# Two state-space convolutions mixed by a gate: the kernels' transform split 64 by 32, doubled rows for one product operation, the gate applied to the inverse's output, the input's spectrum stored once

## The chip, the core and the metric

The kernel runs on one core of a Trainium2 chip. The metric is device time in microseconds (us). Five engines work from queues of their own, each in program order: PE multiplies matrices (the trace shows its weight loads apart, as PEld), DVE and ACT work on vectors and read PE's results in PSUM, POOL works on vectors in SBUF alone, and SP issues every DMA. An engine waits on semaphores for the others, and whatever stands behind a waiting instruction in its queue waits too.

## The reference, cut

Both branches convolve the same input, 2048 positions of 512 channels, with a kernel of 2048 taps that is built from 128 states per channel. A sigmoid of one sum over the channels mixes them.

```python
x = A_u
g = _sigmoid((x * gate_w).sum(-1, keepdims=True))
# branch A (B is alike, with 2 C dt in place of C dt B)
logdA = dt * (A_re + 1j * A_im)
P = jnp.exp(logdA[:, :, None] * l[None, None, :])
K = jnp.einsum("dn,dnl,dn->dl", Cc, P, dB).real
y = irfft(rfft(u, 2 * L) * rfft(K, 2 * L), 2 * L)[:, :, :L] + u * Dskip
...
return g * a + (1 - g) * b
```

## The kernel before

The 512 channels are worked on as eight groups `v` of 64, each with both branches (`k` is 0 or 1); two groups make a quarter `q`. A group takes these steps.

- **Tables** (`chunk`, eight times a group, 16 channels of one branch each). POOL makes the angles `x` (L561, L552) and the magnitudes `E` (L572, L580). ACT takes the sine and the cosine into the PSUM tiles `sd` (L592, L593, L594). DVE multiplies them into `QD` and `E` (L600, L605, L615, L610). PE sums over the 128 states (`products`, L631): per channel 32 by 64 values, four channels side by side in one bank of `ps`. ACT copies two chunks' sums into `K` (L653).
- **The kernel's transform.** `put` is the first stage, a sum over 32 rows per channel (L674), copied into `F` by ACT or DVE (L686). `forward` is the second, over 64 values, with the constant `c_g` (L697).
- **The product** with the input's spectrum `U`: two DVE operations on 128x512, L769 and L772, of which the second takes real and imaginary parts swapped and a sign.
- **The inverse's first stage**: for each frequency column two matmuls that add up, L781 and L782; ACT copies the sum to `st` (L785), and SP stores it to DRAM as `wt` (L788).
- **The inverse's second stage** (`final`, once a quarter): SP loads `wt` back (L803), PE multiplies by `wb` and `wg` (L814), the result is copied (L823 or L825) and stored (L826).

The input's own transform runs once, near the start (`stage1_u`, `stage2_u`): `put` and `forward` for four quarters, then two stores of 128 and 64 rows to `ud` in DRAM (L739), so that a load of `U` (L760) can fetch both row orders. `gate` sums the input over the channels (L843, 512 columns at a time, the same sum in all 128 rows), applies the sigmoid (L854), and POOL multiplies the inverse's constant weights by it (`wg`, L861) and by one minus it (`wb`, L873).

The order on each engine is made before the launch by a planner (`Plan.run`): every operation has an assumed cost and a due time, and whenever an engine is free in the plan, the ready operation with the earliest due time is put next, if the buffers it needs are free in the plan. Due times come from tables (`TO`, `LAG`, `FSP` and others), buffers from `SLOTS`: in PSUM two tiles `sd` of two banks each, for sine and cosine alone, and four banks `ps` for all else.

## Time and profile before

| What | Value |
|---|---|
| Three runs | 503.86 us median, 503.26 to 507.71 |
| The profiled execution | 506.61 us, its span 504.8 us |
| PE, DVE, ACT, POOL busy in the span | 422.9, 398.2, 388.8, 393.8 us |
| DMA, mean | 169 GB/s, 85.45 MB |

An engine's busy time counts a moment once, however many of its instructions overlap. On PE they overlap heavily, so a group's mean duration times its count exceeds its busy time; what a burst costs is read from the starts in the timeline. The trace shows each f32 matmul of the program as two records, each with a weight load of its own: L781 has 256 matmuls in the program and 512 records. The chain of waits goes back from the last instruction, at each step to what released it.

### The profile page before, as it was taken

Reading aid. Unit: us, or ns where it says so; the run is one execution under the profiler, and the core shown is the slowest. Engines: PE = TensorE matmul, PEld = TensorE weight load, DVE = VectorE, ACT = ScalarE, POOL = GpSimd, SP = SyncE. Lnnn points to the kernel's source line nnn. Section 1 sums busy time; section 2 is a strip of 40 time slices with the busy share of each in tenths; the row PEclk is TensorE's granted clock in tenths of the full one; section 3 lists DMA queues with packets and bytes.
Section 4 is the critical chain, followed back from the end, with each engine's and each line's share of the span. In section 5 each row is a group of like instructions: output and inputs, shape, how many; then the busy total and the mean of one; then the engine's idle time right before and its main releaser. Section 6 shows DMA issues by size and latency. Waiting matters only on the chain.

```text
span 504.8 us, 21830 instructions
## 1 busy us (share of the span) xinstructions
PE 422.9 (84%) x9584; PEld 383.2 (76%) x9584; DVE 398.2 (79%) x564; ACT 388.8 (77%) x598; POOL 393.8 (78%) x365
## 2 busy tenths in 40 slices
PE   3497996788989999998289986598999899799946
PEld 3397895777767898888279875488989799789936
DVE  5748998989939889999859988978979999863420
ACT  4659989789999887799998778857999878562111
POOL 4674997979969999989898999768979999920000
PEclk9999997699999999999669999789999999989988
DMA  8958773254654455444208676347336157753954
GB/s 284 382 159 270 225 222 122 86 181 117 153 171 130 138 185 149 127 128 128 62 7 248 197 236 214 107 139 219 106 114 195 34 157 229 218 156 115 307 164 189
DMA packets 69438, 85.45 MB, mean 169 GB/s; under 512 B 4704, under 2 KB 50144, under 8 KB 69088
## 3 DMA queue, kind: packets, MB, share of 16 engines
q1 hardware_dynamic: 69344, 84.06, 53.5%
q8 instruction: 75, 1.23, 1.0%
q14 instruction: 19, 0.16, 0.1%
HBM read 50.49 MB, written 33.59 MB: 167 GB/s over the span
## 4 chain that ended last, share of the span: by engine, by line
PE 45%; ACT 20%; DMA 15%; DVE 8%; issue 7%; POOL 3%; SPq 1%; DVEq 0%; ACTq 0%; POOLq 0%
PE ps L697 10%; PE ps L631 8%; PE ps L781 7%; PE ps L782 7%; PE ps L674 6%; PE ps L814 5%; DMA wt<-st 4%; DMA c_g<-in_c_g 3%; DMA X<-wt 3%; ACT sd L592 3%; ACT sd L594 2%; ACT x L593 2%; DMA AB<-in_prm 2%; ACT st L785 2%; DVE z L772 2%
## 5 line engine op out<-in xcount | busy, mean ns | idle before, releaser
L580 POOL TENSOR_TENSOR E<-AB 128x1024 f32<-128x1024 f32 x64 | 125.4, 1960 | 0.1
L781 PE MATMUL ps<-z,c_t 128*128 128x128 f32 x512 | 102.6, 282 | 3.7 <-DVE z L772 1.6
L782 PE MATMUL ps<-z,c_t 128*128 128x128 f32 x512 | 99.9, 277 | 1.2 <-DVE z L772 0.8
L600 DVE TENSOR_TENSOR QD<-sd,E 128x1024 f32<-128x1024 f32 x64 | 77.8, 1216 | 20.3 <-ACT sd L592 9.4
L631 PE MATMUL ps<-E 128*32 128x64 f32 x2048 | 68.1, 230 | 24.5 <-DVE E L610 17.5
L697 PE MATMUL ps<-F,c_g 128*128 128x128 f32 x640 | 85.7, 281 | 3.5 <-ACT F L686 1.3
L781 PEld LDWEIGHTS ps<-z,c_t 128*128 128x128 f32 x512 | 77.6, 191 | 9.0 <-DVE z L772 3.3
L697 PEld LDWEIGHTS ps<-F,c_g 128*128 128x128 f32 x640 | 77.4, 191 | 8.0 <-ACT F L686 1.6
L782 PEld LDWEIGHTS ps<-z,c_t 128*128 128x128 f32 x512 | 77.7, 192 | 2.8 <-DVE z L772 2.7
L631 PEld LDWEIGHTS ps<-E 128*32 128x32 f32 x2048 | 50.9, 115 | 36.5 <-issue 18.9
L561 POOL TENSOR_TENSOR x<-pi,c_tm 128x512 int32<-128x512 int32 x64 | 68.0, 1064 | 13.1 <-ACT sd L594 12.0
L610 DVE TENSOR_TENSOR E<-sd,E 128x1024 f32<-128x1024 f32 x64 | 77.6, 1213 | 0.8 <-ACT sd L594 0.8
L572 POOL TENSOR_TENSOR E<-AB 128x512 f32<-128x512 f32 x64 | 68.5, 1072 | 8.7 <-issue 2.8
L592 ACT ACTIVATE sd<-x 128x1024 f32<-128x1024 int32 x64 | 65.9, 1030 | 9.0 <-DVE QD L605 7.6
L785 ACT COPY st<-ps 128x512 f32<-128x512 f32 x64 | 37.5, 586 | 44.3 <-PE ps L782 25.1
L552 POOL TENSOR_TENSOR x<-gh 128x512 int32<-128x512 int32 x64 | 68.7, 1074 | 0.2
L593 ACT ACTIVATE x<-x 128x1024 f32<-128x1024 int32 x64 | 67.8, 1060 | 1.3
L594 ACT ACTIVATE sd<-x 128x1024 f32<-128x1024 f32 x64 | 66.0, 1032 | 2.6 <-DVE E L615 0.9
L631 PE MATMUL ps<-QD 128*32 128x64 f32 x2048 | 67.1, 228 | 0.1
L769 DVE TENSOR_TENSOR z<-ps,U 128x512 f32<-128x512 f32 x64 | 43.8, 684 | 27.1 <-PE ps L697 23.7
L631 PEld LDWEIGHTS ps<-QD 128*32 128x32 f32 x2048 | 53.0, 116 | 0.0
L674 PE MATMUL ps<-w,K 64*64 64x64 f32 x2048 | 41.0, 230 | 9.0 <-DVE fi L454 3.4
(118 smaller groups left out, 748.9 us busy)
## 6 DMA issues: line engine op xcount, KB each, us to landing
U<-ud SPq DMA_DIRECT2D x32, 512.0 KB, 4.1
wt<-st SPq DMA_DIRECT2D x64, 256.0 KB, 2.7
X<-wt SPq DMA_DIRECT2D x26, 512.0 KB, 5.6
ud<-z SPq DMA_DIRECT2D x32, 256.0 KB, 3.4
U<-in_u SPq DMA_DIRECT2D x16, 256.0 KB, 4.2
ud<-z SPq DMA_DIRECT2D x32, 128.0 KB, 3.4
U<-in_uT SPq DMA_DIRECT2D x16, 256.0 KB, 3.4
out<-st SPq DMA_DIRECT2D x16, 256.0 KB, 5.7
```

Of the source, the lines that this page charges most:

```text
L552: G.tensor_tensor(xi()[:, :, 1, :].rearrange("n c (a b) -> n c a b", a=4), t[:, :, 0:4].unsqueeze(3).to_broadcast([P, NCK, 4, 8]), t[:, :, ...
L580: G.tensor_tensor(Ev()[:, :, 1:3, :].rearrange("n c w t -> n c (w t)"), AA()[:, ca].rearrange("n c w a -> n (c w) a").unsqueeze(3).to_broa ...
L592: op("A", 0.96, e, lambda: A.activation(bv(sn), wv(xi()), AF.Sin, scale=SCL), r=[x], w=[sn], func="S")
L593: op("A", 0.96, e, lambda: A.activation(x.t, x.v(dt=I32), AF.Abs), w=[x])
L594: op("A", 0.96, e, lambda: A.activation(bv(cs), wv(qv(x)), AF.Sin, bias=HALF_PI, scale=-SCL), r=[x], w=[cs], func="S")
L600: lambda: V.tensor_tensor(ev(QD)[:, :, 0::2, :], bv(sn).rearrange("n w c t -> n c w t"), Ev()[:, :, 0::2, :], ALU.mult),
L610: lambda: V.tensor_tensor(Ev()[:, :, 0:2, :], bv(cs)[:, 0].unsqueeze(2).to_broadcast([P, NCK, 2, NJ]), Ev()[:, :, 0:2, :], ALU.mult),
L631: T.matmul(K4[32 * b : 32 * b + 32, gg, :], ev(QD if w else E)[:, c, 2, :], ev(QD if w else E)[:, c, 0:2].rearrange("n h t -> n (h t)"), s ...
L674: T.matmul(bs[h].t[64 * d : 64 * d + 64, 64 * g : 64 * g + 64], K()[64 * h : 64 * h + 64, 64 * g : 64 * g + 64], w1[64 * h : 64 * h + 64, ...
L697: T.matmul(b.v("p (k m h e) -> p m k h e", k=2, m=4, h=32, e=2)[:, mm], Gw[:, m, :], Fv(F)[:, :, m, :].rearrange("p (k h) e -> p k h e", k=2),
L781: T.matmul(o, Tw[:, m, 0:128], zv(Z1), start=True, stop=False)
L782: T.matmul(o, Tw[:, m, 64:192], zv(Z2), start=False, stop=True)
```

## The change

- **Kernel's transform.** `products` now puts a channel's samples in 64 rows by 32 columns, two halves of 32 rows, with 64 matmuls a chunk in place of 32, each 32 columns wide. `spread` takes the place of `put` for the kernels: a sum over 64 rows, 128 matmuls in place of 32. Its weights `wn` are made on the chip at the start, from loads of `c_w1` and `c_g`.
- **Product.** `forward` uses a copy `Gx` of `c_g` that gives each spectrum row twice, in the layout in which one DVE operation on 128x1024 (`Z`) does the whole product; `U` is loaded into both halves of the partitions.
- **Inverse's first stage.** One matmul of 64 rows per half replaces the pair that added up; its constant `Tx` is cut out of `c_t` by loads whose runs are 32 elements long.
- **Inverse's second stage and gate.** The weights `W` are constant. PE gives the difference of the branches and the second branch in two banks; ACT copies the second, and DVE adds the difference times the gate, four operations of 128x128 a block (L1080). The gate is summed with positions on partitions (256 matmuls one column wide), so that it is a per-partition scalar; the sigmoid is an exponential on ACT and three small operations on DVE. POOL has no part in it.
- **Input's spectrum** is stored once, 128 rows, in 16 stores of 512 KB.
- **Buffers.** `sd` has three tiles of two banks, now also for `spread`, `forward`, `final`, the gate and the parameters; `ps` has two banks. `F` has four tiles, of which one holds `c_g` until the input's transform is done.
- **Last group.** Its two branches are transformed one after the other (`stage2_half`), so that half of its work needs half of its chunks; its spectrum is loaded at once (`load_last`).
- **Tables.** The planner's costs and all due times are other numbers.

```diff
-    "F": (4096, 2), "AB": (28 * NCH, 2), "x": (1024, 2), "E": (1536, 3), "QD": (1536, 2),
-    "K": (512, 2), "z": (512, 4), "U": (1024, 2),
-    "st": (512, 2), "p": (256, 3), "dtb": (256, 2), "pi": (512, 2), "pf": (256, 2), "al": (512, 1), "fi": (256, 2), "gh": (768, 1), "ps": (512, 4), "sd": (1024, 2),
+    "F": (4096, 4), "AB": (28 * NCH, 2), "x": (1024, 2), "E": (1536, 3), "QD": (1536, 2),
+    "K": (512, 2), "z": (1024, 2), "U": (1024, 2),
+    "st": (512, 2), "p": (256, 3), "dtb": (256, 1), "pi": (512, 2), "pf": (256, 2), "al": (512, 1), "fi": (256, 2), "gh": (768, 1), "ps": (512, 2), "sd": (1024, 3),
...
-TO = (-2.668, -0.44, -0.427, -0.242, -0.919, -0.414, 0.283, 2.951)
+TO = (-3.282, -0.921, 0.266, 1.729, 2.552, 2.528, 2.698, 4.476)
...
+    def pair(cls="fd"):
+        b = Buf("sd", cls)
+        return b, [lambda x=x: b.t[:, 512 * x : 512 * x + 512] for x in range(2)]
...
+    Gx = cst.tile([P, NJ, P], F32, tag="Gx", name="Gx")
+    GxB = Buf(None)
+    for x in range(2):
+        for d in range(2):
+            op(
+                "D", 0.5, GXD, lambda x=x, d=d: DMA(Gx[64 * x + 32 * d : 64 * x + 32 * d + 32], ins["c_g"][64 * d : 64 * d + 32]),
+                w=[(GxB, ((2 * x + d, 2 * x + d + 1),))], nbytes=524288,
+            )
...
+    Tx = cst.tile([P, 2, NJ, 64], F32, tag="Tx", name="Tx")
+    TxB = Buf(None)
+    for i, (r, b) in enumerate(((0, 0), (1, 1), (1, 1), (1, 0))):
+        for x in range(2):
+
+            def put_t(i=i, r=r, b=b, x=x):
+                for d in range(2):
+                    DMA(
+                        Tx[32 * i : 32 * i + 32, x].rearrange("p m (d s) -> p m d s", d=2)[:, :, d],
+                        ins["c_t"][64 * r + x : 64 * r + 64 : 2, :, 64 * (b + d) : 64 * (b + d) + 32],
+                    )
+
+            op("D", 1.0, TWD, put_t, w=[(TxB, ((2 * i + x, 2 * i + x + 1),))], nbytes=262144)
...
-                for w in range(2):
-                    for b in range(4):
-                        c = 4 * gg + b
-                        T.matmul(
-                            K4[32 * b : 32 * b + 32, gg, :],
-                            ev(QD if w else E)[:, c, 2, :],
-                            ev(QD if w else E)[:, c, 0:2].rearrange("n h t -> n (h t)"),
-                            start=(w == 0 and gg + ko == 0),
-                            stop=False,
-                        )
+                for e in range(2):
+                    for w in range(2):
+                        for r in range(2):
+                            for h in range(2):
+                                c, o, tb_ = 4 * gg + 2 * r + e, 64 * r + 32 * h, ev(QD if w else E)
+                                T.matmul(
+                                    K4[o : o + 32, gg, e, :],
+                                    tb_[:, c, 2, :],
+                                    tb_[:, c, 1, ::-1] if h else tb_[:, c, 0, :],
+                                    start=(w + e + gg + ko == 0),
+                                    stop=bool(odd and h == 1 and gg + e + w == 5),
+                                )
...
-    def forward(F, mg, due, need=()):
-        b = bank("kh")
+            op("V" if v1 else "A", 0.6 if v1 else 0.51, due, evict, r=[B], w=[(F, ((32 * pos, 32 * pos + 32), allm, (h, h + 1)))])
+
+    def spread(F, K, pos, due, bits):
+
+        B, bs = pair()
 
         def mms():
-            for mm in range(4):
-                m = 4 * mg + mm
-                T.matmul(
-                    b.v("p (k m h e) -> p m k h e", k=2, m=4, h=32, e=2)[:, mm],
-                    Gw[:, m, :],
-                    Fv(F)[:, :, m, :].rearrange("p (k h) e -> p k h e", k=2),
-                    start=True, stop=True,
-                )
-
-        op("T", 0.9, due, mms, r=[(F, (allc, (4 * mg, 4 * mg + 4))), GwB, *need], w=[b])
-        return b
+            for c in range(16):
+                for r in range(2):
+                    for x in range(2):
+                        for d in range(2):
+                            o = 64 * x + 32 * d
+                            T.matmul(
+                                bs[r]()[o : o + 32, 32 * c : 32 * c + 32],
+                                K.t[64 * r : 64 * r + 64, 32 * c : 32 * c + 32],
+                                wn[64 * r : 64 * r + 64, x, d, :],
+                                start=True, stop=True,
+                            )
+
+        op("T", 1.1, due, mms, r=[K, wnB], w=[B], hold=[F])
+        for r in range(2):
+
+            def evict(r=r, e=V.tensor_copy if bits >> r & 1 else A.copy):
+                f = F.t[:, 1024 * pos : 1024 * pos + 1024].rearrange("p (g r m e) -> p r g e m", g=8, r=2, m=NJ, e=2)
+                e(f[:, r], bs[r]().rearrange("p (g e m) -> p g e m", g=8, e=2))
...
+    def forward(F, ug, y, due, need=()):
+        B, bs = pair()
+
+        def mms():
+            for mm, m in enumerate(ms(ug, y)):
+                for r in range(2):
+                    for w in range(2):
+                        for x in range(2):
+                            p, o = slice(64 * x, 64 * x + 64), 64 * r + 32 * w
+                            T.matmul(
+                                bs[x]().rearrange("p (k m h e) -> p m k h e", k=2, m=4, h=32, e=2)[o : o + 32, mm],
+                                Gx[p, m, 64 * r + x : 64 * r + 64 : 2],
+                                Fv(F)[p, :, m, :].rearrange("p (k h) e -> p k h e", k=2),
+                                start=True, stop=True,
+                            )
+
+        op("T", 0.95, due, mms, r=[(F, (allc, allm)), GxB, *need], w=[B])
...
-            op("V", 0.6, dm, lambda Z1=Z1, b=b, uv=uv: V.tensor_tensor(m3(Z1.t), m3(b.t), uv(0), ALU.mult), r=[b, U], w=[Z1], hold=[Z2])
...
-                "V", 0.66, dm,
-                lambda Z2=Z2, b=b, uv=uv: V.scalar_tensor_tensor(m3(Z2.t), m3(b.t), sgn, uv(1), ALU.mult, ALU.mult),
...
-                    T.matmul(o, Tw[:, m, 0:128], zv(Z1), start=True, stop=False)
-                    T.matmul(o, Tw[:, m, 64:192], zv(Z2), start=False, stop=True)
...
+                "V", 1.13, dm,
+                lambda Z=Z, b=b, U=U, y=y: V.tensor_tensor(
+                    Z.t.rearrange("p (x k n) -> p x k n", x=2, k=2), b.t.rearrange("p (x k n) -> p x k n", x=2, k=2),
+                    U.v("p (x y n) -> p x y n", x=2, y=2, n=256)[:, :, y].unsqueeze(2).to_broadcast([P, 2, 2, 256]), ALU.mult,
+                ),
...
+            def mms(ug=ug, y=y, Z=Z, hb=hb):
+                for mm, m in enumerate(ms(ug, y)):
+                    for x in range(2):
+                        T.matmul(
+                            hb.v("p (m k c) -> p m k c", m=4, k=2, c=64)[64 * x : 64 * x + 64, mm],
+                            Tx[:, x, m, :],
+                            Z.v("p (x k m c) -> p x k m c", x=2, k=2, m=4, c=64)[:, x, :, mm, :],
+                            start=True, stop=True,
+                        )
...
+    def stage2_half(k, Ua, due, sp):
+        v = NV - 1
+        F, late = Ft[v], k == 0
+        chans = ((0, 64),) if k else ((64, 128),)
+        for ug in range(4):
+            dm = due + sp * ug / 4
+            Z = Buf(("E", "z")[ug % 2] if late else "z")
+            st, hb = Buf(("st", "QD")[ug % 2] if late else "st"), bank()
+            B, bs = pair("sl" if late else "fd")
...
+                    sets = ((yg, ((1, 0),)), (yb, ((0, 0),))) if lastq else ((yg, ((1, 0), (0, 1))), (yb, ((0, 0),)))
...
+                                            W[:, w, h, :],
...
+                def mix(yg=yg, o=o, bk=bk):
+                    for a in range(4):
+                        V.scalar_tensor_tensor(
+                            at(o.t, a), at(yg(), a), gate_[:, 0, 4 * bk + a : 4 * bk + a + 1], at(o.t, a), ALU.mult, ALU.add
+                        )
...
+                                        y.t[o : o + 32, j : j + 1], tv[:, e, h, b, a], gw[:, q : q + 1],
+                                        start=(sa + q + b + a == 0), stop=(sa == 1 and q == NQ - 1 and j == 15),
```

Three places in the instructions' order follow. In the names, the number behind a tile's name tells its buffer; the size is that of the result. First POOL, where the gate's weights are made, before:

```order
L561 TENSOR_TENSOR x_70<-pi_92,c_tm 128x16x32
L580 TENSOR_TENSOR E_73<-AB_68 128x16x64
L861 TENSOR_TENSOR wg<-X,w1i 128x4x32 x16
L873 TENSOR_TENSOR X<-w1i,wg 128x4x32 x8
L506 TENSOR_TENSOR AB_68<-AB_68,pf_94 128x128x4
L873 TENSOR_TENSOR X<-w1i,wg 128x4x32 x4
L461 TENSOR_TENSOR p_89<-pi_92,c_tm 128x256
L465 TENSOR_TENSOR fi_97<-fi_97,p_89 128x256
```

The corresponding stretch after the change, in which the same quarter's parameters are finished (angles `x` at L666 and L657, magnitudes `E` at L677 and L685):

```order
L685 TENSOR_TENSOR E_74<-AB_70 128x16x64
L637 TENSOR_TENSOR gh_98<-pi_92,c_tm 128x768
L647 TENSOR_TENSOR gh_98<-gh_98,fi_96 128x64x4
L559 TENSOR_TENSOR fi_96<-fi_96,p_87 128x256
L677 TENSOR_TENSOR E_75<-AB_70 128x16x32
L685 TENSOR_TENSOR E_75<-AB_70 128x16x64
L598 TENSOR_TENSOR AB_71<-AB_71,pf_93 128x128x4
L666 TENSOR_TENSOR x_72<-pi_92,c_tm 128x16x32
```

The 32 operations for the weights are gone, and the tables follow each other.

Second DVE, from the last chunk's last operation to its products in the last group, before:

```order
L610 TENSOR_TENSOR E_72<-sd_105,E_72 128x16x64
L769 TENSOR_TENSOR z_81<-ps_100,U_84 128x512
L772 SCALAR_TENSOR_TENSOR z_82<-ps_100,sgn,U_84 128x512
L686 COPY F_67<-ps_102 128x8x64
L769 TENSOR_TENSOR z_79<-ps_100,U_83 128x512
L772 SCALAR_TENSOR_TENSOR z_80<-ps_100,sgn,U_83 128x512
L769 TENSOR_TENSOR z_81<-ps_101,U_83 128x512
L772 SCALAR_TENSOR_TENSOR z_82<-ps_101,sgn,U_83 128x512
```

And after (L705 to L715 are the last chunk's):

```order
L705 TENSOR_TENSOR QD_78<-sd_101,E_74 128x16x2x32
L710 SCALAR_TENSOR_TENSOR QD_78<-sd_101,E_74 128x16x32
L720 TENSOR_TENSOR E_74<-sd_102,E_74 128x16x32
L715 TENSOR_TENSOR E_74<-sd_102,E_74 128x16x64
L822 COPY F_69<-sd_101 128x8x2x32
L999 TENSOR_TENSOR z_81<-sd_103,F_66 128x1024
L999 TENSOR_TENSOR z_82<-sd_102,F_66 128x1024
```

All eight products of the last group (L999) now stand behind the last copy into `F`; the six not shown follow these two directly, and then the gate's operations (L1080).

Third PE, near the end, before (second stage, then the first stage of the inverse):

```order
L781 MATMUL ps_103<-z_81,c_t 128x128
L782 MATMUL ps_103<-z_82,c_t 128x128
L697 MATMUL ps_101<-F_67,c_g 128x2x64 x4
L697 MATMUL ps_100<-F_67,c_g 128x2x64 x4
L781 MATMUL ps_102<-z_79,c_t 128x128
L782 MATMUL ps_102<-z_80,c_t 128x128
```

And after (`spread` is L810, the second stage L987, the inverse's first stage L1006, its second L1059):

```order
L810 MATMUL sd_101<-wn,K_80 32x32 x128
L1006 MATMUL ps_99<-z_82,Tx 64x64 x16
L987 MATMUL sd_103<-F_69,Gx 32x64 x64
L987 MATMUL sd_102<-F_69,Gx 32x64 x64
L987 MATMUL sd_101<-F_69,Gx 32x64 x64
L1006 MATMUL ps_100<-z_81,Tx 64x64 x16
```

A burst has more and smaller matmuls, and the pairs that added up are single matmuls of 64 rows.

## The prediction on record

> **What bounds the kernel now.** I read the busy times first, then the busy time by stretch of the span. Columns of the second view are the stretch, its length, busy time of PE, PEld, DVE, ACT and POOL, each with its count, then PE's granted clock, DMA's share and GB/s.
>
> ```profile
> PE 422.9 (84%) x9584; PEld 383.2 (76%) x9584; DVE 398.2 (79%) x564; ACT 388.8 (77%) x598; POOL 393.8 (78%) x365
> 0.00:50.00 50.00, 31.54 (x746) 29.08 (x747) 32.61 (x68) 32.77 (x71) 28.72 (x36) 1.00 0.80 275
> 50.00:450.00 400.00, 349.00 (x8254) 313.90 (x8253) 349.06 (x474) 343.44 (x508) 365.10 (x330) 0.94 0.51 154
> 450.00:505.00 55.00, 42.38 (x602) 40.19 (x594) 16.52 (x24) 12.62 (x21) 0.00 (x0) 0.94 0.54 180
> ```
>
> Over the span PE leads, but by stretches it does not: from 50 to 450 POOL is busy 365.1 of 400 us, the others 343 to 349, and after 450 POOL has nothing left. So the span is two parts: the time until POOL has made the last table, and what must follow that. The timeline gives the border, and the chain of waits shows that four engines take turns on the way to it:
>
> ```profile
> PE 45%; ACT 20%; DMA 15%; DVE 8%; issue 7%; POOL 3%; SPq 1%; DVEq 0%; ACTq 0%; POOLq 0%
> 445.84 1.95 POOL L580 TENSOR_TENSOR E<-AB 128x1024 f32<-128x1024 f32 x1
> ```
>
> POOL ends at 447.8: 393.8 of work and 54.0 of waiting. Then come 504.8 - 447.8 = 57.0 us of tail. I price the change in these two parts, after asking whether another engine takes POOL's place.
>
> **PE, part by part.** The bursts as they are:
>
> ```profile
> 50.84 1.10 PE ps L631 x64
> 52.27 1.09 PE ps L674 x64
> 445.06 0.39 PE L782 MATMUL ps<-z,c_t 128*128 128x128 f32 x2
> 445.28 0.39 PE L781 MATMUL ps<-z,c_t 128*128 128x128 f32 x2
> 452.42 0.39 PE L814 MATMUL ps<-X,wg 128*64 128x128 f32 x4
> 452.64 0.39 PE L814 MATMUL ps<-X 128*64 128x128 f32 x4
> L843 PE MATMUL ps<-U,gate_w 128*128 128x512 f32 x32 | 17.2, 625 | 2.9 <-DMA U<-in_uT 2.7
> ```
>
> A full-array matmul, 128 columns wide, starts every 0.22 us (445.06, 445.28); two matmuls of 64 rows, side by side, take the same 0.22 (452.42, 452.64). So:
> - Inverse, first stage: 8 full matmuls a block, 1.78 us, become 8 of 64 rows in pairs, 4 x 0.22 = 0.89. Over 64 blocks: -57 us.
> - `forward`: 32 matmuls of a 64 by 32 piece, eight side by side, 4 x 0.22 = 0.89, as 4 full ones today. Nothing.
> - `final`: three sets of 16 matmuls, four side by side, 12 x 0.22 = 2.64 for 12 blocks, 1.76 for 4, against 1.76 for each of 16 now: 12 x 0.88 = +10.6.
> - The gate's sum: 17.2 now; 256 matmuls of one column then. What bounds those is how fast records start.
>
> For that I narrow the timeline to the first nanoseconds of one burst; the answers are for stretches that begin at 311.80 and end at 311.81, 311.83 and 311.86:
>
> ```profile
> 311.80 0.11 PEld L631 LDWEIGHTS ps<-E 128*32 128x32 f32 x1
> 311.80 0.13 PEld L631 LDWEIGHTS ps<-E 128*32 128x32 f32 x4
> 311.80 0.16 PEld L631 LDWEIGHTS ps<-E 128*32 128x32 f32 x8
> ```
>
> One, four and eight loads have begun after 10, 30 and 60 ns: a record starts every 7 ns or so. `products`: 64 matmuls, 128 records, 128 x 7 ns = 0.9 us, and about 0.2 to start and drain as in the 1.10 above (its columns alone, 32 of 128 at four side by side, need 16 x 0.055 = 0.88): 1.1, nothing to +0.1 a chunk; I take +3 us in all. The gate: 512 x 7 ns = 3.6, with eight starts about 5: -12. `spread` is the open price. Eight pieces side by side would stream its 128 matmuls in 16 x 0.055 = 0.88 us; at 7 ns its 256 records take 1.8. Ends: 1.1 (no change, if pieces in different rows start twice as fast) and 2.0. I take 2.0, since L674, which has pieces in different rows too, shows no faster start than 64 records in 1.09: 32 x 0.9 = +29. PE's sum is -57 + 10.6 - 12 + 29 + 3 = -26: 397 us. It stays beside POOL, not above it.
>
> **DVE, ACT, POOL.**
>
> ```profile
> L600 DVE TENSOR_TENSOR QD<-sd,E 128x1024 f32<-128x1024 f32 x64 | 77.8, 1216 | 20.3 <-ACT sd L592 9.4 <-POOL E L580 4.2 <-PE ps L631 3.5
> L769 DVE TENSOR_TENSOR z<-ps,U 128x512 f32<-128x512 f32 x64 | 43.8, 684 | 27.1 <-PE ps L697 23.7 <-PE ps L781 1.3 <-ACT x L593 0.9
> L772 DVE SCALAR_TENSOR_TENSOR z<-ps,sgn,U 128x512 f32<-128x512 f32 x64 | 47.3, 741 | 0.0
> L732 DVE COPY z<-ps 128x512 f32<-128x512 f32 x20 | 13.7, 685 | 9.7 <-PE ps L697 9.5
> L823 DVE COPY st<-ps 128x512 f32<-128x512 f32 x6 | 4.1, 692 | 4.6 <-PE ps L814 4.3 <-DMA wt<-st 0.4
> L443 DVE SCALAR_TENSOR_TENSOR pf<-ps,dtb 128x128 f32<-128x128 f32 x4 | 1.2, 291 | 0.1
> L854 ACT ACTIVATE X<-X 128x2048 f32<-128x2048 f32 x1 | 1.9, 1914 | 0.0
> L361 ACT COPY dtb<-ps 128x128 f32<-128x128 f32 x4 | 1.0, 260 | 1.4 <-PE ps L353 1.4
> L861 POOL TENSOR_TENSOR wg<-X,w1i 128x128 f32<-128x128 f32 x16 | 6.7, 457 | 0.0
> L873 POOL TENSOR_TENSOR X<-w1i,wg 128x128 f32<-128x128 f32 x16 | 6.8, 467 | 0.0
> ```
>
> DVE: the product falls from 43.8 + 47.3 to 64 x 1.216 = 77.8, -13.3. The gate adds 64 operations of L443's form, 64 x 0.291 = +18.6, and L823's copies go, -4.1. The tables of who copies give DVE 44 of the copies into `F` (39 now), 5 x 0.685 = +3.4, and 8 double ones of the input's spectrum (9.7) for 20 (13.7), -4.0. In sum +0.6: 399 us. ACT: 16 pieces of L361's size, +4.2, two copies more at the output, +1.2, five fewer into `F`, -2.9, sigmoid -1.9, the four copies of the gate's sums -2.3, input's spectrum +1: no change. So neither is relieved, and a PE that is 26 us shorter does not by itself end anything sooner.
>
> POOL loses L861 and L873: -13.5. It gains six operations of 64 elements for `wn`, at most 6 x 0.457, at least a third of that; I take +1.6. That is -12, and all of it lies in POOL's busiest part.
>
> POOL's 54 us of waiting I leave as it is. What would shorten it is a PE that holds ACT up less; what would lengthen it are the three `sd` tiles (a rival below). The start I also take as even.
>
> ```profile
> 8.00 17.61 DMA c_g<-in_c_g
> 14.28 3.12 POOL L572 TENSOR_TENSOR E<-AB 128x512 f32<-128x512 f32 x3 [2.22 <-ACT AB L490]
> ```
>
> In SP's queue `Gx` puts 2 MB ahead of `c_g`, but the 3.1 MB of `c_t` that stood ahead of it go behind, as `Tx` with its short runs, which only the first inverse block needs; the input's 1 MB goes ahead of the parameters. Bounds: 11 us less, if `c_g` gains all of 3.1 MB at the first stretch's 275 GB/s; 11 more, if POOL's first `E`, at 14.3 now, has to wait for its loads until 25.6, when `c_g` lands now.
>
> So POOL ends at about 447.8 - 12 = 436.
>
> **The tail.** What follows POOL's end now:
>
> ```profile
> 450.43 1.21 DVE L600 TENSOR_TENSOR QD<-sd,E 128x1024 f32<-128x1024 f32 x1
> 476.52 0.59 ACT L785 COPY st<-ps 128x512 f32<-128x512 f32 x1 [8.19 <-DMA wt<-st]
> 485.30 0.59 ACT L785 COPY st<-ps 128x512 f32<-128x512 f32 x1 [1.20 <-PE ps L782]
> 492.40 0.70 PE L814 MATMUL ps<-F,X 128*64 128x128 f32 x4 [7.19 <-DMA F<-wt]
> 501.25 0.58 ACT L825 COPY st<-ps 128x512 f32<-128x512 f32 x1 [1.16 <-PE ps L814]
> ```
>
> Today PE still owes two groups, and ACT waits 8.19 us for a store to free `st`. After the change four of the last eight blocks go to other tiles, half of the group's forward work may run before the last chunks, and the order shows one path: DVE finishes the chunk (2.6 us after POOL's end, as now, then 1.2 + 0.7 + 0.7 + 1.2 = 3.8), `products` 1.1, copy `K` 0.6, `spread` 2.0, copy into `F` 0.7, then all eight products on DVE, 8 x 1.216 = 9.7, one inverse block and its copy 1.5. From 485.9 to 492.4 the last store and load take 6.5, which stays. Four blocks of `final` 7.0 (8.9 now, at a cold clock), the last block's ACT and DVE pieces 4 x 0.26 + 4 x 0.29 = 2.2, the last store 504.8 - 501.8 = 3.0. Sum 40.7, and ten hand-overs of about 0.2: 43, against 57.
>
> **The sum.** 436 + 43 = 479 of span. The execution takes 506.6 where its span is 504.8, so 480.8; the runs' median lies 2.75 below that execution. Forecast: 478 us. Its own range, 11 us either way for the start and 3 for the tail's hand-overs and `spread`, is 464 to 492.
>
> **Rivals.**
> - *PE sets ACT and DVE free.* Their three longest waits are on it; POOL waits on ACT for 12.7 and 12.0:
>
> ```profile
> ACT st L785 <- PE ps L782: 25.1, 18, 3.6
> DVE z L769 <- PE ps L697: 23.7, 16, 4.2
> ACT st L825 <- PE ps L814: 20.7, 7, 10.1
> POOL AB L506 <- ACT AB L492: 12.7, 6, 4.4
> POOL x L561 <- ACT sd L594: 12.0, 7, 3.5
> ```
>
> If `spread` costs 1.1, PE is at 368, and half of POOL's 24.7 goes: 478 - 12 = 466. For it: 25.1 + 23.7 + 20.7 = 69.5 us of waits on PE. Against: POOL's longer one follows five activations in a row, which stay.
> - *Three PSUM tiles for everything* (slower than now). Sine and cosine each hold a tile from ACT's start to DVE's end:
>
> ```profile
> 381.67 1.03 ACT L592 ACTIVATE sd<-x 128x1024 f32<-128x1024 int32 x1 [0.73 <-DVE QD L605]
> 384.36 0.68 DVE L605 SCALAR_TENSOR_TENSOR QD<-sd,E 128x512 f32<-128x512 f32 x1
> ```
>
> At the least that is 1.03 + 1.21 + 0.68 = 2.9 us; here it is 385.04 - 381.67 = 3.4. With all users: 128 x 2.9, 64 forwards x 2.1, 32 spreads x 2.7, 32 copies of the input's transform x 2.5, 16 finals x 4.4 = 742 us, on three tiles 247, from about 26 us on. At 3.4/2.9 = 1.15 times that the tiles are held 284 of 436 us, and nothing stands. The tiles become the bound where the mean hold passes 1.65 times the least, and the kernel is slower than now past 1.94; at twice, 26 + 494 = 520. The gate, which keeps one tile until its last load, speaks for it.
> - *The start eats it.* POOL's first `E` waits for `wn`, and so for loads of 8-byte runs behind `Gx`. Were that at 25.6, as above, and the tail's gain halved, 478 + 11 + 7 = 496; with PE behind as well, within 1% of 504.
> - *Small matmuls bound PE.* The change has 12,808 matmuls, so 25,616 records for 9,584. If each took the mean of a whole burst today, 1.03 us for 64 = 16 ns, `products` would cost 2.1 and `spread` 4.1: 64 + 96 us over their cheap ends, PE at 528, and over 600 us in all. The three rows of loads above speak against it: eight began in 60 ns. The Trainium skill, TensorE: Matmul & The Clock Gate, section "Wait — 56ns, not 53.3ns?", says that matmul starts never come closer than about 25 ns however few columns there are; by that the records alone would take 640 us, an estimate. The trace does not agree for pieces side by side.
>
> **How the numbers follow.** Forecast 0.68, PE sets free 0.13, three tiles 0.10, the start 0.07, small matmuls 0.02. About 1% is what a measurement of this kernel can tell from no change: 499 to 509. Faster: 0.68 + 0.13 and a little of the start's, 0.82; within: 0.06; slower: 0.10 + 0.02, 0.12. The range leaves out the lowest part of the second case and both slow ones: 456 to 502.
>
> **What would show it.** Right: POOL's last operation near 436 with its busy time near 382, 43 us from there to the end, the inverse's first stage at 0.9 us a block, `spread` near 2 us with PE near 397, DVE unchanged at 399. Wrong: POOL's last operation later than 450 with waits of ACT and PE on DVE's release of `sd` (three tiles), a first `E` after 20 us (the start), or `products` over 1.5 us (small matmuls). If `spread` takes 1.1, the second case is the likelier.

## The result, and the profile after

The changed kernel takes 914.38 us, median of 4 runs (909.98 to 923.70); the kernel before takes 505.78 (503.26 to 507.78) in four. The ratio is 1.805, its 95% interval 1.790 to 1.821: slower by 409 us where the prediction had 28 us faster. The ratio leaves out the slow execution of 923.70. The profiled execution took 911.88 us, its span 910.0.

From the page of the kernel before, one row that the prediction did not read: the queue that fetches instructions, with its packets, MB and share.

```profile
q8 instruction: 75, 1.23, 1.0%
```

The page of the changed kernel: busy times, the same row, and the chain of waits.

```profile
PE 563.1 (62%) x25616; PEld 490.6 (54%) x25616; DVE 446.2 (49%) x558; ACT 454.9 (50%) x603; POOL 421.5 (46%) x339
q8 instruction: 200, 3.28, 1.5%
PE 46%; issue 32%; DVE 9%; ACT 5%; DMA 2%; POOL 1%; SPq 1%; DVEq 0%; ACTq 0%; POOLq 0%
```

No engine is busy for two thirds of the span. A third of the chain is "issue": time in which an engine waited for nothing that the profile shows. Matmuls and weight loads are 51,232 instructions, and 200 packets of 16 KB are one for each 256 of them; before there were 75 for 19,168, the same quotient.

The stretches between the start and POOL's end, and from there to the end (columns as in the prediction), and POOL's last operation:

```profile
50.00:450.00 400.00, 254.80 (x11865) 224.13 (x11861) 208.13 (x256) 212.56 (x279) 205.40 (x164) 0.73 0.30 89
801.00:910.00 109.00, 65.21 (x3168) 59.02 (x3153) 26.49 (x47) 21.03 (x39) 0.35 (x1) 0.69 0.30 83
```

```profile
799.38 1.96 POOL L685 TENSOR_TENSOR E<-AB 128x1024 f32<-128x1024 f32 x1
```

POOL ends at 801.3, not at 436, and 108.7 us follow, not 43. From 50 to 450 the vector engines work half the time, where each had 343 to 365 us of 400. The longest waits:

```profile
POOL x L666 <- ACT sd L699: 184.4, 32, 18.9
PEld sd L810 <- issue: 130.4, 62, 4.8
POOL E L677 <- PE ps L736: 122.5, 26, 11.2
DVE z L931 <- PE sd L856: 113.1, 29, 10.0
ACT F L822 <- PE sd L810: 98.3, 17, 9.4
PEld ps L736 <- issue: 89.3, 76, 4.4
```

Most of the others wait for PE, and PE and its loads wait for "issue", in `spread` (L810) and `products` (L736). The timeline of one `spread` shows how:

```profile
647.52 1.20 PE L810 MATMUL sd<-wn,K 64*32 64x32 f32 x96
650.74 1.32 PE L810 MATMUL sd<-wn,K 64*32 64x32 f32 x128 [2.02 <-issue]
655.31 0.45 PE L810 MATMUL sd<-wn,K 64*32 64x32 f32 x27 [3.25 <-issue]
```

Its 256 records come in portions of at most 128, each nearly as fast as the prediction said (128 in 1.3 us), with stalls of 2 to 3 us between them. 128 records and their 128 loads are the 256 instructions of one packet. The whole burst takes 8.5 us. From a burst's first start to its last end the median is 6.78 for `spread`, 2.50 for a chunk's `products` (mean 2.85, the shortest 1.29) and 2.14 for a block's `forward`. Of the 56 bursts of `forward` 39 have no gap over 0.3 us between starts and still take 2.07, so its length has another cause, to which a later section comes.

The trace also has the queue's packets one by one. Most of these packets take 0.9 to 1.4 us. Call it a stall of PE when more than 0.3 us pass between the starts of one record or load and the next: there are 247, together 395 us. Of these, 151 end 1.1 to 1.65 us after a packet has landed, and they sum to 287.8 us; if stalls and packets had nothing to do with each other, 30 stalls and 48 us would fall there. In the kernel before it is 16 stalls and 17.1 us, where chance gives 8 and 8.4 us. Two packets follow one another by 3.4 us at the least in the kernel before and by 3.3 in the changed one. Before, the median distance is 5.3 us, after it is 3.9.

### The profile page after: what moved, and what is told of

It reads as the page before. It is cut to its first block, busy times and chain, and to the rows that moved or that the text cites. A ratio compares the mean times of both kernels' runs of the same rounds, so it can differ in the third digit from the quotient of the medians.

```text
span 910.0 us, 53877 instructions
## 1 busy us (share of the span) xinstructions
PE 563.1 (62%) x25616; PEld 490.6 (54%) x25616; DVE 446.2 (49%) x558; ACT 454.9 (50%) x603; POOL 421.5 (46%) x339
## 4 chain that ended last, share of the span: by engine, by line
PE 46%; issue 32%; DVE 9%; ACT 5%; DMA 2%; POOL 1%; SPq 1%; DVEq 0%; ACTq 0%; POOLq 0%
PE sd L810 11%; PE ps L736 10%; PE sd L856 6%; PE ps L941 6%; PE sd L1059 4%; PE sd L837 3%; DVE E L715 2%; PE sd L987 2%; PE sd L783 2%; DVE z L931 2%; DVE QD L705 1%; PE ps L1006 1%; DVE E L720 1%; ACT sd L699 1%; PE sd L1113 1%
## 5 line engine op out<-in xcount | busy, mean ns | idle before, releaser
L810 PE MATMUL sd<-wn,K 64*32 64x32 f32 x8192 | 99.8, 228 | 130.8 <-issue 119.1
L810 PEld LDWEIGHTS sd<-wn,K 64*32 64x32 f32 x8192 | 89.5, 127 | 141.8 <-issue 130.4
L666 POOL TENSOR_TENSOR x<-pi,c_tm 128x512 int32<-128x512 int32 x64 | 72.5, 1132 | 193.0 <-ACT sd L699 184.4
L677 POOL TENSOR_TENSOR E<-AB 128x512 f32<-128x512 f32 x64 | 86.7, 1356 | 131.7 <-PE ps L736 122.5
L931 DVE TENSOR_TENSOR z<-sd,U 128x1024 f32<-128x1024 f32 x56 | 82.4, 1492 | 128.0 <-PE sd L856 113.1
L685 POOL TENSOR_TENSOR E<-AB 128x1024 f32<-128x1024 f32 x64 | 138.4, 2162 | 0.0
L856 PE MATMUL sd<-F,Gx 64*32 64x128 f32 x3584 | 117.4, 392 | 26.2 <-issue 18.4
L736 PE MATMUL ps<-E 128*32 128x32 f32 x4096 | 105.2, 219 | 43.3 <-issue 28.6
L736 PE MATMUL ps<-QD 128*32 128x32 f32 x4096 | 104.7, 218 | 40.7 <-issue 40.5
L736 PEld LDWEIGHTS ps<-E 128*32 128x32 f32 x4096 | 94.0, 131 | 56.8 <-issue 46.9
L736 PEld LDWEIGHTS ps<-QD 128*32 128x32 f32 x4096 | 94.5, 131 | 42.4 <-issue 42.4
L856 PEld LDWEIGHTS sd<-F,Gx 64*32 64x32 f32 x3584 | 85.8, 129 | 46.3 <-issue 29.9
L705 DVE TENSOR_TENSOR QD<-sd,E 128x1024 f32<-128x1024 f32 x64 | 85.6, 1338 | 26.6 <-ACT sd L697 16.5
L715 DVE TENSOR_TENSOR E<-sd,E 128x1024 f32<-128x1024 f32 x64 | 91.4, 1428 | 11.0 <-ACT sd L699 10.9
L941 PE MATMUL ps<-z,Tx 128*64 128x128 f32 x896 | 82.4, 340 | 18.4 <-DVE z L931 6.5
L941 PEld LDWEIGHTS ps<-z,Tx 128*64 128x64 f32 x896 | 65.0, 172 | 32.4 <-ACT st L949 12.1
```

The lines of the kernel that those rows point to most:

```text
L677: G.tensor_tensor(Ev()[:, :, 0, :].rearrange("n c (a b) -> n c a b", a=4), A1()[:, ca, ::-1].unsqueeze(3).to_broadcast([P, NCK, 4, 8]), BB ...
L685: G.tensor_tensor(Ev()[:, :, 1:3, :].rearrange("n c w t -> n c (w t)"), AA()[:, ca].rearrange("n c w a -> n (c w) a").unsqueeze(3).to_broa ...
L705: lambda: V.tensor_tensor(ev(QD)[:, :, 0::2, :], bv(sn).rearrange("n w c t -> n c w t"), Ev()[:, :, 0::2, :], ALU.mult),
L715: lambda: V.tensor_tensor(Ev()[:, :, 0:2, :], bv(cs)[:, 0].unsqueeze(2).to_broadcast([P, NCK, 2, NJ]), Ev()[:, :, 0:2, :], ALU.mult),
L736: T.matmul(K4[o : o + 32, gg, e, :], tb_[:, c, 2, :], tb_[:, c, 1, ::-1] if h else tb_[:, c, 0, :], start=(w + e + gg + ko == 0), stop=boo ...
L810: T.matmul(bs[r]()[o : o + 32, 32 * c : 32 * c + 32], K.t[64 * r : 64 * r + 64, 32 * c : 32 * c + 32], wn[64 * r : 64 * r + 64, x, d, :], ...
```

## The experiments

Times without an interval are single executions. The kernel before took 502.7 to 511.4 us on the chips that were used, and a run that edits it is compared with the time on its own chip; runs that edit the changed kernel are set against its 914.38 us.

**Theory:** PE gets 256 instructions in about 3.5 us, that is 128 records at 27 ns each, however short they are, and the change multiplied the records. **Rivals:** the array cannot take the small pieces side by side; three PSUM tiles hold everything up; the start.

### Pieces by themselves

PE alone, seven stretches of 1,024 small matmuls:

```diff
+ b[i % 2][o : o + 32, c : c + cols] <- k[r : r + 64, 32 columns], w[r : r + 64, c : c + cols]   # r 0/64, o 0/32/64/96 in turn
+ stretches: cols 32, 16, 64; 128 rows and 32 columns; 32 beside 2 MB loads; 32 beside copies; 32
```

> No convolution: PE alone, 1,024 matmuls (2,048 records) in each of seven stretches, after 256 full ones. Pieces of 64 by 32 with 32, 16 and 64 columns, pieces of 128 by 32 with 32 columns, then 32 columns again beside loads of 2 MB, beside copies on DVE, ACT and POOL, and alone. Supply of instructions: 25 to 28 ns a record in all of them, 50 to 57 us a stretch, with a fetch of 16 KB for each 256 instructions of PE, and perhaps longer beside the loads. Columns that pass one piece after another: 16 columns half of that, 64 twice. Start rate of the bursts that the forecast used: 7 ns a record, 15 us a stretch.

The timeline, for each stretch first and last of the portions used: 32 columns, 16, 64, and 32 beside the loads.

```profile
69.85 2.12 PE L56 MATMUL b<-w,k 64*32 64x32 f32 x223 [1.80 <-DVE b L93]
...
81.02 1.53 PE L56 MATMUL b<-w,k 64*32 64x32 f32 x128 [1.92 <-issue]
...
120.66 1.53 PE L56 MATMUL b<-w,k 64*32 64x32 f32 x128 [1.92 <-issue]
...
132.12 1.43 PE L56 MATMUL b<-w,k 64*32 64x16 f32 x128 [2.57 <-issue]
...
175.76 1.43 PE L56 MATMUL b<-w,k 64*32 64x16 f32 x128 [2.02 <-issue]
...
194.95 2.04 PE L56 MATMUL b<-w,k 64*32 64x64 f32 x128 [2.26 <-issue]
...
238.32 2.04 PE L56 MATMUL b<-w,k 64*32 64x64 f32 x128 [1.69 <-issue]
...
309.09 1.53 PE L56 MATMUL b<-w,k 64*32 64x32 f32 x128 [4.41 <-issue]
...
340.15 1.54 PE L56 MATMUL b<-w,k 64*32 64x32 f32 x128 [4.67 <-issue]
```

A portion of 128 starts every (120.66 - 81.02) / 11 = 3.60 us with 32 columns, 43.64 / 12 = 3.64 with 16 and 43.37 / 12 = 3.61 with 64: 28 ns a record, and the columns only shift time between portion and stall. With pieces of 128 rows it is 3.63. So the array is not what limits. Nor is it the clock: 0.50 to 0.55 was granted in these stretches, and the distance is close to the shortest one between packets in the two kernels (3.4 and 3.3 us) at clocks of 0.95 and 0.75. Of the run's 117 stalls 110 end 1.1 to 1.65 us after a packet has landed. What had been fetched ahead was gone after the first 223 records. Beside loads at 380 GB/s the distance is 31.06 / 5 = 6.21 us, 49 ns a record. The packets themselves take 1.0 us there as without loads, but follow one another later; why is not shown. Copies on the vector engines made no such difference (3.86 us, and 3.77 in the last stretch without them).

### The changed kernel with twice the columns in `spread`, as many records

```diff
-   bs[r]()[o : o + 32, 32 * c : 32 * c + 32], K.t[..., 32 * c : 32 * c + 32], wn[..., x, d, :]
+   bs[r]()[o : o + 32, c1 : c1 + 64],         K.t[..., 32 * c : 32 * c + 32], wn[..., x] (64 columns)
```

> The changed kernel with each of the first stage's matmuls on 64 columns in place of 32 (half of what it writes is written again by the next): as many records, twice the columns. Supply of instructions: 914 us within 2%. Pieces that pass through the array one after another, 128 x 0.055 us more in each of 32 bursts: +225, about 1,140 us; eight side by side and bound by their columns: +28, about 940. Tiles: no change but what a longer burst holds.

911.43 us. Twice the columns cost nothing, which speaks against the array.

### Small pieces merged into wide ones

```diff
- K4[o : o + 32, gg, e, :], tb_[:, c, 2, :], ...      # 64 a chunk
+ K4[o : o + 64, gg, e, :], tb_[:, c, 1:3, :], ...    # 32 a chunk
- bs[r]()[o : o + 32, ...], K.t[..., 32 columns], wn[..., x, d, :]
+ bs[r]()[:, ...], K.t[..., 128 columns], wn[..., 0, 0, :]
```

> The changed kernel with neighbouring small pieces merged into wider ones: products 32 matmuls of 64 rows a chunk in place of 64, the kernels' first stage 32 of 128 rows in place of 128, forward 8 in place of 32, the inverse's second stage and the gate's sum a quarter. The merged pieces get the wrong operands; tiles, their users, DVE, ACT, POOL and DMA stay as they are. About 10,400 records on PE in place of 25,616. Supply of PE's instructions (16 KB, 256 instructions, every 3.5 us or so): 460 to 510 us. Pieces that do not stream side by side in the array: 460 to 510 too. Three PSUM tiles for everything, or the start: 880 to 920 us.

748.85 us: 166 less, but no theory had that figure. The merged pieces get other operands, so the result is not the kernel's. The groups:

```profile
L807 PE MATMUL sd<-wn,K 64*128 64x32 f32 x2048 | 164.0, 325 | 7.6 <-ACT K L761 2.7
L735 PE MATMUL ps<-E 128*64 128x32 f32 x2048 | 159.1, 252 | 12.0 <-DVE E L720 8.9
```

The "issue" waits fall to 4% of the chain, but PE is busy 656.5 of 746.5 us. By the starts within a burst, 32 columns through a piece of 128 columns took 55 ns a record where the granted clock was 1.0 and 105 where it was 0.5, and through one of 64 columns 29 and 53, where narrow pieces side by side start every 7. Merging traded one limit for another. It does not part the theories, but shows that the number of matmuls alone does not set their price.

### The kernel before with more records

Each matmul of `products` cut into four of 16 columns, first with the four parts of a channel behind one another, then with neighbouring matmuls in different places:

```diff
  for w in range(2):
-     for b in range(4):
-         T.matmul(K4[32 * b : 32 * b + 32, gg, :], ..., 64 columns)
+     for h in range(4):
+         for b in range(4):                      # first run: b outside, h inside
+             T.matmul(K4[32 * b : 32 * b + 32, gg, 16 * h : 16 * h + 16], ..., 16 columns)
```

> The kernel before with each matmul of products cut into four of 16 columns: same result, same columns streamed, same tiles, and 12,288 records more (21,872). Supply of instructions at 27 ns a record: 590 us at the least, 620 to 700 with what it waits for besides. Pieces bound by their columns in the array: 506 us, no change. Three PSUM tiles: no change, since this kernel's tiles are as before.

> The kernel before with each matmul of products cut into four of 16 columns, as the run of quarters did, but with neighbouring matmuls in four different places of the array: same result, same columns streamed, same tiles, 21,872 records. Supply of instructions at 27 ns a record (the pieces alone took 27 whatever their columns): 256 records 6.9 us a chunk in place of 1.1, with other work of PE between filling up what was fetched ahead: 780 to 890 us, and stalls of 1.5 to 2.5 us every 128 records. Columns in the array: 1.1 us a chunk as before, 506 to 520. Three PSUM tiles: 506.

888.71 and 852.13 us. The first run is above its range, since parts in the same place wait for each other: a record took 26 ns there without any stall, so it does not part the theories. The second does. Its page:

```profile
PE 602.8 (71%) x21872; PEld 554.9 (65%) x21872; DVE 399.1 (47%) x564; ACT 392.4 (46%) x598; POOL 395.8 (47%) x365
q8 instruction: 171, 2.80, 1.4%
PE 63%; issue 25%; DMA 5%; DVE 4%; ACT 2%; POOL 1%; SPq 1%; DVEq 0%; ACTq 0%
```

Same columns, same tiles, same order, DVE, ACT and POOL as busy as before, and 345 us more: 12,288 records at 28 ns. That is a loss of the change's size, made in the kernel before by records alone.

### The changed kernel with fewer, longer matmuls

Each piece keeps its size and place, and the columns through the array stay about the same. In the first run this is done everywhere, then in `spread` alone, then in `products` alone:

```diff
- spread:   16 c x 8 matmuls of 32 columns
+ spread:    4 c x 8 matmuls of 128 columns
- products: 64 of 32 columns        + 32 of 64
- forward:  32 of 128 columns       + 16 of 256    (final and gate likewise)
```

> The changed kernel with its small matmuls half as many and twice as long (products 64 columns, forward 256, the inverse's second stage 256, the gate's sum 2; the kernels' first stage a quarter, 128 columns), each piece as large and where it was, with operands of other channels or columns. As many columns through the array, tiles, DVE, ACT, POOL and DMA as they are; about 12,100 records in place of 25,616. Supply of instructions: 480 to 560 us. Columns in the array, three PSUM tiles for everything, or the start: 890 to 930.

> The changed kernel with that change in the kernels' first stage alone: 32 matmuls of 128 columns in place of 128 of 32, 6,144 records fewer, operands of other channels. Supply of instructions: a burst of 6.9 us falls to 2, 32 x 4.9 = 157 us less, 740 to 790 in all. Columns in the array, tiles: 890 to 930.

> The changed kernel with that change in products alone: 32 matmuls of 64 columns a chunk in place of 64 of 32, 4,096 records fewer, one of two channels' operands left out. Supply of instructions: 3.5 us a chunk falls to 1.1 to 1.75, 64 x 1.75 to 2.4 = 110 to 150 us less, 760 to 810 in all. Columns in the array, tiles: 890 to 930.

566.68 (7 us over its range), 726.31 and 819.51 us. `spread` alone gives 188 us (the theory: 157) and `products` alone 95 (110 to 150), so both sizes were off, and the direction was not. The bursts of `spread` got 155 us shorter in the first, and in the second those of `products` 60 and of `spread` another 26; one packet can hold the end of one burst and the start of the next. 13,504 records fewer in all are worth 348 us, 26 ns each. Tiles, start, DVE's and ACT's operations are the same in these runs, and so they are not what these 348 us were lost to.

### What lengthens the vector engines' operations

In the changed kernel DVE, ACT and POOL are also busy 40 to 66 us longer than forecast. The medians of their operations are as before, but some last 1 to 2 us longer, on all three engines in the same stretches. Summed over the medians it is 177 us on the three, and 158 of these lie in operations that overlap `forward` (L856). Two things are new there: it reads `F` eight pieces at a time, in runs of 8 bytes, and it loads every second column of `Gx`.

```diff
  Gx[p, m, 64 * r + x : 64 * r + 64 : 2],                  # second run: 32 neighbouring columns
- Fv(F)[p, :, m, :]                                        # 64 runs of 8 bytes, 256 bytes apart
+ F.t[p, 128 * m : 128 * m + 128]                          # first run: one run of 512 bytes
```

> The changed kernel whose forward reads its 128 columns of F in one run of 512 bytes a row, in place of 64 runs of 8 bytes 256 bytes apart; columns of other frequencies, everything else as it is, 25,616 records. Theory: the eight pieces' reads of F in short runs hold up every engine that reads or writes SBUF; then operations of DVE, ACT and POOL that fall in forward's bursts last as long as the others (L931's mean 1,225 ns in place of 1,492, the excess over the medians under 15 us summed over the three engines, 158 in the changed kernel), and the time falls by what of it lay on the path, 20 to 60 us: 850 to 895. Supply of instructions alone: 914 within 2%, long operations as before. Strided weights: no change.

> The changed kernel whose forward loads 32 neighbouring columns of Gx as weights in place of every second one (rows of other frequencies), F read as it is. Reads of F in short runs: L931's mean 1,492 ns as it is, the time 914 within 2%. Strided weights: 1,225 and 850 to 895.

895.28 and 910.04 us. DVE's product (L931) in the changed kernel, in the first run and in the second, and `forward` itself in the changed kernel and in the first run:

```profile
L931 DVE TENSOR_TENSOR z<-sd,U 128x1024 f32<-128x1024 f32 x56 | 82.4, 1492 | 128.0 <-PE sd L856 113.1
```

```profile
L931 DVE TENSOR_TENSOR z<-sd,U 128x1024 f32<-128x1024 f32 x56 | 68.3, 1222 | 128.8 <-PE sd L856 109.6
```

```profile
L931 DVE TENSOR_TENSOR z<-sd,U 128x1024 f32<-128x1024 f32 x56 | 83.1, 1506 | 123.6 <-PE sd L856 106.0
```

```profile
L856 PE MATMUL sd<-F,Gx 64*32 64x128 f32 x3584 | 117.4, 392 | 26.2 <-issue 18.4
```

```profile
L856 PE MATMUL sd<-F,Gx 64*32 64x128 f32 x3584 | 86.0, 324 | 33.3 <-issue 31.3
```

With long runs the mean is the median again (1,222 ns), the excess falls from 177 us to 3, and the time by 19 us, just short of the 20 to 60 expected. That is 15 us beside the second run on the same chip, one execution each; by either, most of the excess was not on the path. PE itself is held up too: a burst of `forward` without a stall takes 1.29 us with long runs, where it took 2.07. The weights make no difference. With matmuls by themselves, each stretch beside 16 copies on every vector engine:

> No convolution: 16 copies of 128 by 1024 on each of DVE, ACT and POOL at the same time, beside PE: nothing; 128 full matmuls that read 64 runs of 8 bytes a row; 512 pieces of 64 by 32, eight places in turn, that read 64 runs of 8 bytes; the same with 32 runs of 16 bytes; the same with one run of 512 bytes. If short runs read by pieces hold up the vector engines: copies 30 to 60% longer in the third stretch, less in the fourth, none in the fifth and second. If any read in short runs does: the second stretch too. If it is something else in forward: no stretch.

The timeline: full matmuls that read runs of 8 bytes and ACT's copies beside them; eight pieces that do, and the copies of the three engines beside those; the same pieces with one run a row, and ACT.

```profile
51.34 31.67 PE L43 MATMUL b<-k 128*128 128x128 f32 x256 [26.32 <-DVE b L71]
51.40 10.77 ACT L80 COPY v<-v 128x1024 f32<-128x1024 f32 x10
84.31 29.73 PE L56 MATMUL b<-k 64*32 64x128 f32 x1024 [1.30 <-DVE b L71]
84.44 27.72 DVE L80 COPY v<-v 128x1024 f32<-128x1024 f32 x1
84.37 29.92 ACT L80 COPY v<-v 128x1024 f32<-128x1024 f32 x2
84.43 30.26 POOL L80 COPY v<-v 128x1024 f32<-128x1024 f32 x2
184.15 5.36 ACT L80 COPY v<-v 128x1024 f32<-128x1024 f32 x5
```

The effect was expected at 30 to 60%. It is a standstill: for 29.7 us of pieces DVE finishes one copy, ACT and POOL two, where a copy takes 1.05 us on ACT and 1.4 on DVE beside POOL. Full matmuls that read the same runs do nothing of the kind, nor do pieces with long runs; with runs of 16 bytes some copies took two to three times as long.

### Both causes away

The run of fewer, longer matmuls with `F` read in one run, and then with the matmuls once more half as many:

```diff
- products: 32 of 64 columns   + 16 of 128
- forward:  16 of 256          + 8 of 512      (input's first stage 128, final 512)
```

> The kernel with half as many, twice as long matmuls (566.7 us), whose forward also reads F in one run a row. If reads of F in short runs hold up the vector engines: excess of 59 us summed over them to under 10, POOL's busy time from 395 to about 382, the time to 520 to 555. If with both causes gone the rest of the forecast holds (POOL done near 436, 43 us behind it): 480 to 510. If three PSUM tiles are the bound by then: 550 to 570, with waits of ACT and PE on DVE's release of sd.

> The kernel of both cuts (558.8 us, 12,112 records), its small matmuls once more half as many and twice as long: products 128 columns, the input's first stage 128, forward 512, the inverse's second stage 512, the gate's sum 4. As many columns through the array, tiles and vector engines as they are; about 7,700 records. If the rest of the time over the forecast is still supply of instructions: 495 to 530 us, and waits of PE on issue fall to half. If it is the three PSUM tiles, the order or the tail: 550 to 560.

558.82 and 508.72 us. The first is above the 520 to 555 expected and lies where three PSUM tiles as the bound would have put it, 81 us over the forecast. The second decides against the tiles, which are as before, and lies where supply put it, 50 us lower. Most of these 50 were supply: stalls that end as above after a packet's landing fall from 64.0 us to 19.4, where chance gives 20 and 16. The page of the second, its stretch up to 450, and POOL's last operation:

```profile
PE 361.4 (71%) x7920; PEld 241.9 (48%) x7920; DVE 401.4 (79%) x558; ACT 391.3 (77%) x603; POOL 381.6 (75%) x339
q8 instruction: 62, 1.02, 0.9%
```

```profile
50.00:450.00 400.00, 304.87 (x6770) 203.75 (x6772) 356.42 (x462) 343.60 (x501) 354.49 (x301) 0.93 0.55 161
```

```profile
449.06 1.96 POOL L685 TENSOR_TENSOR E<-AB 128x1024 f32<-128x1024 f32 x1
```

The vector engines are full again, POOL ends at 451.0 and the tail is 55.4 us.

### The kernel before with fewer records

First with 128 columns in `put`, half of them of other rows, then with the same result by a sum over all 128 rows, and that for the input alone:

```diff
- bs[h].t[64 * d : 64 * d + 64, 64 g], K()[64 * h : 64 * h + 64, 64 g], w1[64 * h : ..., d, 64 * h : ...]
+ bs[h].t[64 * d : 64 * d + 64, 64 g and 64 (g + 1)], K()[64 * h : ...], w1[64 * h : ..., d]              # first run
+ bs[g // 4].t[64 * d : 64 * d + 64, 128 * (g % 4) ...], K()[:, 64 g], w1[:, d, :]                      # second and third
```

> The kernel before whose first stage has half as many matmuls, 128 columns long in place of 64 (half of what they write is of other rows), 1,536 records fewer of 9,584. If the kernel before lost time to the supply of instructions already (its waits on issue sum to some 45 us): 492 to 502 us. If it did not: 505 within 1%.

> The kernel before, same result, whose first stage sums over all 128 rows at once with the weights' zero blocks: 16 matmuls of 128 by 64 on 128 columns in place of 32 of 64 by 64 on 64, 1,536 records fewer, twice the columns' time in the array, 0.8 us more in each of 48 bursts where instructions are there. Supply of instructions limits the kernel before: the 6 us that halving the records alone gave, less what of 48 x 0.8 = 38 us of PE work lies on the path: 496 to 512. Array alone: 508 to 520.

> That change for the input's first stage alone, at the start, where transfers fill the queues and a fetch takes longest: 512 records fewer, 16 bursts 0.8 us longer in the array. Supply of instructions: 500 to 505, 0 to 4 us faster; array alone: 505 to 510.

Ratios to the kernel before: 0.987 (0.979 to 0.995), 1.019 (1.014 to 1.023) and 1.012 (1.006 to 1.017). 1,536 records fewer give 1.3%, some 6 us. Stalls of 9 us above chance in the kernel before would allow that, but the 48 bursts of `put` also got 0.06 us shorter each, 3 us in all, and the runs do not part the two. With the same result they are bought with time in the array, and 4 to 9 us are lost, as the array alone had it. So no version here with the same result beats the kernel before.

## Why the prediction was wrong

- **The step that failed** is "a record starts every 7 ns or so". It was read from eight loads in 60 ns, and holds within a portion of 128 records. As a rate for the kernel it is wrong by four: one portion follows the last after 3.5 us. With it fell the prices of `products` (1.1 us a chunk; measured 2.50, past the 1.5 that the prediction named as a sign) and of `spread` (2.0; 6.78). For what the array alone has to do, PE's sum of 397 us was high rather than low: 361 in the run with the fewest records, whose chunk takes 1.08 and whose `spread` takes 1.16, near the cheap end of 1.1.
- **A second price failed by itself: `forward`** ("Nothing", 0.89 us; measured 2.14). Here it is less the supply than the reads of `F` in runs of 8 bytes, which the prediction priced like any other: 1.29 us without a stall once the runs are long (by starts alone, as 0.89 was counted, 1.72 and 1.02).
- **The rival "small matmuls bound PE"** had the right quantity, the number of records, and a chance of 0.02. It was dismissed by the rows of the loads, which lie within one packet. Its price of 16 ns a record came from bursts of 64, which end before the supply does. What would have priced it stood in the record: the page has 75 packets for 9,584 records, so 200 for 25,616, and at the 3.4 us that two packets were apart at the least in the kernel before, that is 680 us, an estimate.
- The Trainium skill, Runtime: NRT & Kernel Launch, section "Instruction fetch mechanics", describes blocks of 16 KiB, 256 instructions, and calls the cost of crossing one mostly hidden. The runs agree on the block; hidden it was not: 288 us of stalls here. The floor of about 25 ns between starts that the prediction quoted from the Trainium skill, TensorE: Matmul & The Clock Gate, and set aside is near the 28 ns that held on the mean, though single starts within a portion came 7 ns apart; whether the two figures have one origin is not shown.
- **DVE, ACT and POOL.** Forecast 399, no change from 389, and 382; measured 446, 455 and 422. Without the stalls and the short runs they are 401, 391 and 382, so the counts were right, and what the prediction missed is that `forward`'s reads hold up the three.
- **The clock** that PE was granted fell as well, from 0.94 to 0.73 in the stretch from 50 to 450, and no term had that. The inverse's first stage, with the same matmuls, is busy 82.4 us in the changed kernel at a mean clock of 0.75 and 62.9 in the run with the fewest records at 0.92. What the lower clock cost on the path was not separated; it was back at 0.92 in the run of fewer, longer matmuls, in which nothing else had changed.
- **The start** was taken as even, with 11 us either way. It came out at the late end, past the 20 us that the prediction named as the sign of its rival "the start eats it", and by the path named there: POOL makes `wn` first and waits for its loads.

```profile
20.79 0.57 POOL L319 COPY w<-z 128x128 f32<-128x128 f32 x2 [3.02 <-DMA z<-in_c_w]
22.52 0.32 POOL L363 TENSOR_TENSOR wn<-z 128x64 f32<-128x64 f32 x1 [1.16 <-DMA z<-in_c_g]
...
24.95 1.06 POOL L677 TENSOR_TENSOR E<-AB 128x512 f32<-128x512 f32 x1
```

  POOL's first `E` is at 24.95, 10.7 us later than before; in the run with both causes away it is at 26.62. That start is 12 us late, beside the 15 by which POOL's end at 451 misses 436.
- **The tail** is 55.4 us in that run, for 43. By its timeline, 26.6 go until the last block's copy ends (about 24 in the sum's terms), 13.0 until the last blocks of `final` start, behind the store and the load (6.5), 12.7 for these blocks and their pieces (9.2, at a granted clock of 0.71) and 3.1 for the last store (3.0). Why the store and the load took twice as long was not tried.
- **Three PSUM tiles** and **PE sets ACT and DVE free:** with the causes away, the same tiles and order reach 508.7 us, 2.7 under the kernel before in one run each. The tiles do not explain the loss; a few us of theirs may lie in what is left, which stays open. So the 28 us forecast are not there even without the two causes. The span of that run, 506.4 us, is 27 us over the 479 of the forecast's sum, 15 up to POOL's end and 12 behind it; this part failed apart from supply.
- **The inverse's first stage** is near its price: from a block's first start to its last the median is 0.86 us, for 0.89. **The gate's sum** waits on issue too (9.3 us in its loads), which is small beside the rest.

## What to carry to other kernels

Count PE's instructions before the columns: in these runs 256 of them, 128 matmul records with their loads, came once in 3.5 us and beside heavy transfers once in 6.2, so a burst of short matmuls longer than what is fetched ahead runs at 28 to 49 ns a record whatever the array could do. Packing small matmuls side by side pays only while each keeps the array busy as long as its instructions take to come, which eight pieces with 64 columns did not yet (2.04 of 3.6 us, at a granted clock of about 0.5). The packets of the instruction queue, at 3.4 us each, set beside the span, say how near a kernel is to this limit: 255 of 505 us before, 680 of 910 after. A rate read within nanoseconds is no rate for a stage.

## What was not expected of the hardware

Eight pieces of PE that read SBUF in runs of 8 bytes nearly stopped three other engines that used other tiles: one copy in 27.72 us on DVE where 1.41 is usual, and no effect with full matmuls or with runs of 512 bytes. The Trainium skill, SBUF — State Buffer, section "Who interferes with whom", names the port pair of the vector and GpSimd engines as the only place of contention; ACT, which has no part in it, stood still here too, and so the measurement decides. Why reads by pieces differ from reads by the whole array was not tried.
